# Attention and two mixture layers on one core: the gate tiles are moved by 384 bytes, and TensorE gets filler matmuls in the first stage

## The chip, the cores and the metric

The kernel runs on 1 core of one Trainium2 chip. The metric is the device time of one execution in microseconds (us); the kernel before has a median of 1256.49 us over 3 runs (1256.25 to 1257.84).

## What is computed

The reference is linear attention over 4 batches, 8 heads, 576 positions and 64 channels, then a feed-forward layer on 2304 tokens (512 to 2048 to 512), then four experts (512 to 1024 to 512) whose results are summed with the weights of `domain_probs`. Cut to what matters:

```python
q_s = softmax(q, axis=-1);  k_s = softmax(k, axis=2)
x = q_s @ (k_s.T @ v)                    # per head, heads side by side: 2304 x 512
h = x @ w_in                             # w_in and w_out arrive in float64
g = where(h >= 1, h, where(h <= -1, 0, (h + 1) ** 2 / 4))
x = g @ w_out
for e in range(4):
    out += p[:, e:e+1] * (maximum(x @ w1[e], 0) @ w2[e])
```

## The kernel before, in words

Tokens are cut into five blocks (512, 512, 512, 256, 512). They run in two passes: blocks 1 and 0, then blocks 2, 4 and 3. In each pass the first layer comes first ("a") and the four experts follow ("b"). Each product of two matrices is made of three matmuls of rounded parts, high and low, in `products` (lines 998, 999 and 1000): the low weight part with the high moving part, high with low, high with high. So nearly all of TensorE's time stands under these three lines. Most products of two blocks are made with seven products in place of eight (`strassen`); the first layer of the first pass is made plainly, by `ups` (line 1121 and on).

The hidden values of a step are written as a pair of tiles, high and low, that the program calls gates. `gated` (lines 1322 to 1351) does it for the first layer, `opened` (line 1308 and on) for the experts; then `downs` (line 1353 and on) multiplies them with the second weights. For the first layer a gate is the moving operand and the weight is loaded into the array ("bank<-gate,w" in the trace, moving operand first). For the experts the gate is loaded and the weight moves ("bank<-w,gate").

Three sets of tiles serve as gates. Halves of spare `x` tiles serve at first. Eight tiles named `gate` come when the conversion of the float64 weights is over: `end_conversion` (line 343) closes the pool `convert` and opens the pool `gates` in its place, on the right side of the memory (lines 352 to 354). Ten tiles named `gate_late` come when the attention is over. They lie on the left side.

Where the tiles lie follows from the allocation. Left-side pools are stacked from low addresses up, right-side pools from the top down. In the program before, the tiles `x`, `acc`, `w`, `cv`, `words` and `gate_late` all start 96 bytes past a multiple of 512 in each partition. The right-side pool is 16,384 bytes long and starts at byte 212,960, which is 480 past a multiple of 512. In it lie, first, `words1`, `m1` and `t1` of the conversion, and later the eight `gate` tiles of 2,048 bytes each, so each `gate` tile starts at 480, too.

The first stage holds the attention of batches 0 and 1 (`load_units`, `keys`, `queries`), the conversion of float64 weights on VectorE and ScalarE (`split_double`, lines 675 to 727) and the first steps of the first layer. TensorE's order is not written by hand: every piece of work is a generator that asks for an engine and a cost, for a buffer, or for an event. `Order.run` keeps a clock for each engine in the computed order, and always lets the request go on that can start first; among requests for the same engine that can start within 0.05 of the first, the one with the lowest due number goes. The order found so is the order of the instructions on each engine. `order.now` is the computed time. An estimate of the costs is in the code: a matmul of n columns costs 0.0135 + n / 2400 per pass, and a hop between engines 0.2.

`ups` writes to the banks of `ups_banks`. At first there are two of them (line 359); two more come when batch 1 and when all batches are done. `ups` takes its bank at the start of a step, before its weights and its x are there, and `gated` gives it back after the VectorE instruction of line 1340. A generator that asks for a buffer while one is free gets it at once:

```python
        elif isinstance(want, Bufs) and want.free:
            time, item = want.take()
            self.hold(task, time)
            self.go_on(task, item)
```

In the trace a float32 matmul of the program (as in lines 819, 823, 920 and 921) shows as two records, x2.

Of the kernel before, what the change touches and what calls it, by code (L numbers as in the profile page):

```python
# [8 lines left out]
F32 = mybir.dt.float32  # L9
# [8 lines left out]
P = 128  # L18
EPS = 1e-9

PE, ACT, DVE, POOL, SP = "PE", "ACT", "DVE", "POOL", "SP"
# [155 lines left out]
def act(n, psum=False):  # L177
    return ACT, (0.14 if psum else 0.17) + n * 0.00087


def dve(n):
    return DVE, 0.14 + n * 0.00107
# [15 lines left out]
def attention_moe_kernel(  # L198
# [12 lines left out]
    nc = tc.nc  # L211
# [43 lines left out]
    steps = [(g, j) for g, (bi, ws) in enumerate(groups) for j in range(len(ws))]  # L255
# [18 lines left out]
    QRATIO = 9.0  # L274
    MARGIN = 0.5
    POOLRATIO = 3.0
    CORDER = range(KC)

    def bufs(pool, n, shape, dtype, name):
        return [pool.tile(shape, dtype, name=f"{name}{i}") for i in range(n)]  # L280
# [5 lines left out]
    ident = const.tile([P, P], F32, name="ident")  # L286
# [18 lines left out]
    for i, (_, n) in enumerate(blocks):  # L305
# [12 lines left out]
    at_first = convert.enter_context(tc.tile_pool(name="convert", bufs=1, side="right"))  # L318
# [5 lines left out]
             xtiles.pop()),  # L324
        )
    ])
    xfree = Bufs([])
    first_gates = [(x[:, i * 512:(i + 1) * 512], x) for x in xtiles for i in range(2)]
    gate_home = {id(g): x for g, x in first_gates}
# [4 lines left out]
    def give_gate(g, t):  # L334
        x = gate_home.get(id(g))
        if not switched or x is None:
            gates.put(g, t)
        elif id(x) in halves_in:
            xfree.put(x, max(t, halves_in.pop(id(x))))
        else:  # L340
            halves_in[id(x)] = t

    def end_conversion(t):

        switched.append(True)
        free, gates.free = gates.free, []
        for t0, _, g in free:
            give_gate(g, max(t, t0))
        for t0, _, x in made_of.free:
            xfree.put(x["f"], max(t, t0))  # L350
        convert.close()
        pool = ctx.enter_context(tc.tile_pool(name="gates", bufs=1, side="right"))
        for x in bufs(pool, 8, [P, 512], F32R, "gate"):
            gates.put(x, t)
        for i in range(3):
            raws.put(words[:, i * 512:(i + 1) * 512], t)

    banks = bufs(psum, 8, [P, 512], F32, "bank")
    ups_banks = Bufs(banks[:2])
# [61 lines left out]
    order = Order()  # L421

    def end_attention(t):
        early.close()
        late = ctx.enter_context(tc.tile_pool(name="late", bufs=1))
        for x in bufs(late, 10, [P, 512], F32R, "gate_late"):
            gates.put(x, t)
        ups_banks.put(banks[6], t)
# [14 lines left out]
    def token_rows(t, t0, n):  # L443

        done = 0
        while done < n:
            b, s = divmod(t0 + done, S)
            place, p = (1 + s // P, s % P) if s < (NC - 1) * P else (0, s - (NC - 1) * P)
            m = min(n - done, HP - p % HP)
            rows = t[b * S:(b + 1) * S]  # L450
            if p < HP:
                rows = rows[:HP * NC].rearrange("(p c) d -> c p d", c=NC)[place, p:p + m]
            else:
                p -= HP
                rows = rows[HP * NC:].rearrange("(p c) d -> c p d", c=NC - 1)[place - 1, p:p + m]
            yield done, m, rows
            done += m
# [3 lines left out]
    def norm_probs():  # L461
        start = Event()
        start.set(150.0)
        yield start
        for i in range(NT // P):
            for o, n, rows in token_rows(probs, i * P, P):
                t = yield SP, 0.65
                nc.sync.dma_start(out=pn[o:o + n, i, :], in_=rows)
        late = Event()
        late.set(t + 3)  # L470
        yield late
        t = yield dve(300)
        nc.vector.tensor_reduce(out=psum_p, in_=pn, axis=AX.X, op=ALU.add)
        nc.vector.tensor_scalar(out=psum_p, in0=psum_p, scalar1=EPS, scalar2=None, op0=ALU.add)
        nc.vector.reciprocal(out=psum_p, in_=psum_p)
        nc.vector.tensor_tensor(
            out=pn, in0=pn, in1=psum_p.unsqueeze(2).to_broadcast([P, NT // P, NE]), op=ALU.mult
        )
        probs_in.set(t)
# [21 lines left out]
    def load_weights():  # L501
        for ws in jobs:
            w = ws[0]
            yield step_of[w][0]
            if is_kept(w):
                for h in range(2):
                    for w in ws:
                        raw = yield raws
                        raw_of[w, h] = raw
                        t = yield SP, 0.48  # L510
                        nc.sync.dma_start(
                            out=f32(raw).rearrange("p (z n) -> p z n", z=2), in_=kept[w[:3]][:, :, h]
                        )
                        loaded[w, h].set(order.arrival(t, 4096))
                continue
            kind, e, f = w[:3]
            n = P * len(ws)
            both = (yield wide_raws) if kind == "a" else None
            a, c = (w_in, w_out) if kind == "a" else (w1[e], w2[e])
            fs = slice(f, f + n)  # L520
            for h, src in enumerate((
                a[:, fs].rearrange("(c p) f -> p c f", p=P), c[fs].rearrange("(c p) d -> p c d", p=P)
            )):
                if kind == "a":
                    raw_of[w] = both
                    raw = both[:, h * 512:(h + 1) * 512]
                else:
                    raw_of[w, h] = yield raws
                    raw = f32(raw_of[w, h])
                t = yield SP, 0.48  # L530
                nc.sync.dma_start(
                    out=raw.rearrange("p (c f) -> p c f", c=KC if h == 0 else len(ws)), in_=src
                )
                loaded[w, h].set(order.arrival(t, 4096))
# [140 lines left out]
    def split_double(w, cv):  # L675
# [49 lines left out]
        if not to_convert:  # L725
            end_conversion(at_time)
# [45 lines left out]
    def load_units():  # L772
        for b, hp in todo:
            yield att_due[b, hp] - 0.1
            hs = slice(2 * hp, 2 * hp + 2)
            if (b, hp) == (1, 0):
                yield GATE
            if (b, hp) == (NOW, 0):
                yield calm
            small = yield k_small  # L780
            kt = yield wide
            k_at = Event()
            k_at.set((yield from load(places(kt), k[b, hs])))
            ek = yield wide
            order.add(keys(b, hp, small, kt, ek, k_at), "att", att_due[b, hp])
            small = yield q_small
            qt = yield wide
            q_at = Event()
            q_at.set((yield from load(places(qt), q[b, hs])))
            order.add(queries(b, hp, small, qt, q_at), "att", att_due[b, hp])  # L790

    def keys(b, hp, small, kt_buf, ek_buf, k_at):
# [39 lines left out]
        else:  # L832
            yield pe(P, 2)
            nc.tensor.transpose(bank[:, P:2 * P], mc.to_broadcast([P, P]), ident)
            rows, way = bank[:, P:2 * P], dve(W)
            if order.busier(DVE, POOL, POOLRATIO):
                t, e = yield [act(P, True), dve(P)]
# [56 lines left out]
    def queries(b, hp, small, qt_buf, q_at):  # L894
# [98 lines left out]
        if len(done) == len(todo):  # L993
            end_attention(t)


    def products(ps, ah, al, bh, bl, first, last, **kw):
        nc.tensor.matmul(ps, al, bh, start=first, stop=False, **kw)  # L998
        nc.tensor.matmul(ps, ah, bl, start=False, stop=False, **kw)  # L999
        nc.tensor.matmul(ps, ah, bh, start=False, stop=last, **kw)  # L1000
# [112 lines left out]
    def prepare_all():  # L1113
        for i in range(len(PASSES)):
            if i:
                yield from prepare(i, "a")
            yield from prepare(i, "b")
# [235 lines left out]
    def downs():  # L1353
        s0 = 0
        for g, (bi, ws) in enumerate(groups):
# [4 lines left out]
            if kind == "a" and bi == PASSES[0][0][1] and g == place[-1]:  # L1360

                each = [x for x in each if x[0] < 2] + [(j, c) for c in CORDER for j in range(2, nj)]
            ps, left, begun = {}, [m] * nj, [0] * m
# [68 lines left out]
    with tc.manual_schedule():  # L1432
        make_identity(nc, ident)
        nc.gpsimd.tensor_scalar(
            out=nident, in0=ident, scalar1=-1.0, scalar2=None, op0=ALU.mult
        )
        nc.gpsimd.memset(half, 0.5)
        nc.scalar.activation(out=one, in_=half, func=AF.Exp, scale=0.0)
        nc.gpsimd.memset(rebias, -8.0 * ((1023 - 127) << 20))
        for free in kvbds:  # L1440
            for _, _, t in free.free:
                nc.gpsimd.memset(t, 0.0)
        order.clock[POOL] = 3.0
        order.add(load_units(), "load")
        order.add(load_weights(), "load")
        order.add(convert_weights(), "conv")
        order.add(downs(), "ffn")
        order.add(ups(), "ffn")
        order.add(prepare_all(), "ffn")
        order.add(norm_probs(), "load", len(steps))  # L1450
        order.run()


# [30 lines left out]
```

## Time and profile before

| | us |
|---|---|
| median of 3 runs | 1256.49 |
| the profiled execution, its own time | 1260.49 |
| its span, first to last instruction | 1258.7 |
| TensorE (PE) busy | 1222.2 (97%) |
| VectorE (DVE) busy | 668.7 (53%) |
| GpSimd (POOL) busy | 568.7 (45%) |
| ScalarE (ACT) busy | 510.7 (41%) |

The page of the profile gives these for one execution. TensorE's matmuls are pipelined, so the duration of one record overlaps the next; the distance from one start to the next tells what a matmul costs. The granted clock of TensorE is given as a share of full speed: 1.00 is 2.4 GHz and 0.50 is 1.2 GHz. Before the first change of the clock that the profile recorded (at about 16 us), the clock column shows 1.00 whatever the clock was.

### The profile page before, as it was taken

To read this page: it belongs to the slowest core of one execution; us is meant where nothing else is said; L and a number is where in the kernel's file an instruction comes from. 1 tells how busy PE (TensorE), PEld (TensorE's weight loads), DVE (VectorE), ACT (ScalarE), POOL (GpSimd) and SP (SyncE) were. 2 spreads that over 40 slices of the span, in tenths; PEclk is the share of its full clock that TensorE was granted. 3 is DMA by queue.
4 is the path that set the end of the run, shared out by engine and by line. 5 is a ranking of instruction groups with operands and counts; after the bars stand their busy time and mean duration, and the time that the engine had idled before them with its cause. 6 is when DMAs were issued, how large, how long until landed. Compare 5 with 4: busy or idle time off the path is not lost.

```text
span 1258.7 us, 15378 instructions
## 1 busy us (share of the span) xinstructions
PE 1222.2 (97%) x5716; PEld 1001.8 (80%) x5716; DVE 668.7 (53%) x1030; ACT 510.7 (41%) x918; POOL 568.7 (45%) x559
## 2 busy tenths in 40 slices
PE   6789999989999999999999999999999999999998
PEld 3568888867778878888788888888888888888886
DVE  5878885467564654445553455673334333343333
ACT  3657765343433433323574443533223223232220
POOL 1323233465744645533673745748334253342500
PEclk9999999999999999999999999999999999999999
DMA  7856754114232212111531221202011010111003
GB/s 184 242 159 201 237 199 151 34 38 119 83 86 86 78 55 78 36 66 35 140 127 67 99 74 63 67 1 72 32 65 34 34 51 22 63 34 34 17 1 84
DMA packets 86218, 105.37 MB, mean 84 GB/s; under 512 B 28544, under 2 KB 61312, under 8 KB 86144
## 3 DMA queue, kind: packets, MB, share of 16 engines
q1 hardware_dynamic: 86144, 104.39, 26.8%
q8 instruction: 45, 0.74, 0.2%
q14 instruction: 29, 0.24, 0.1%
HBM read 82.87 MB, written 21.50 MB: 83 GB/s over the span
## 4 chain that ended last, share of the span: by engine, by line
PE 88%; DVE 5%; DMA 3%; issue 1%; POOL 1%; ACT 1%; SPq 1%; DVEq 0%; POOLq 0%; ACTq 0%
PE bank L998 28%; PE bank L999 28%; PE bank L1000 28%; DMA acc<-in_v_dram 1%; PE bank L867 1%; PE bank L962 1%; DVE acc L440 1%; DMA wide<-in_q_dram 1%; POOL w L440 1%; DMA acc<-in_k_dram 1%; DVE x L440 0%; PE bank L952 0%; DMA acc<-in_q_dram 0%; SPq L758 0%; ACT w L435 0%
## 5 line engine op out<-in xcount | busy, mean ns | idle before, releaser
L998 PE MATMUL bank<-x,w 128*128 128x512 f32 (+1 forms) x988 | 372.6, 377 | 8.0 <-DVE w L710 3.6
L999 PE MATMUL bank<-x,w 128*128 128x512 f32 (+1 forms) x988 | 366.4, 371 | 3.2 <-DVE x L440 1.1
L1000 PE MATMUL bank<-x,w 128*128 128x512 f32 (+1 forms) x988 | 366.0, 370 | 0.0
L440 POOL TENSOR_TENSOR w<-words,w 128x512 fp32r<-128x512 f32 (+1 forms) x128 | 159.3, 1248 | 248.3 <-ACT w L435 247.5
L998 PEld LDWEIGHTS bank<-x,w 128*128 128x128 f32 x988 | 187.0, 189 | 45.6 <-DVE w L710 4.3
L999 PEld LDWEIGHTS bank<-x,w 128*128 128x128 f32 x988 | 187.0, 189 | 37.1 <-DVE x L440 2.2
L1000 PEld LDWEIGHTS bank<-x,w 128*128 128x128 f32 x988 | 186.8, 189 | 31.9
L1422 DVE SCALAR_TENSOR_TENSOR acc<-bank,pn,acc 128x512 f32<-128x512 f32 x126 | 88.6, 749 | 133.7 <-PE bank L1000 133.7
L435 ACT CAST w<-words 128x512 fp32r<-128x512 f32 (+2 forms) x160 | 106.8, 681 | 84.3 <-PE bank L1000 67.1
L998 PE MATMUL bank<-w,gate 128*128 128x512 f32 x344 | 138.6, 403 | 0.6 <-DVE gate L1315 0.6
L999 PE MATMUL bank<-w,gate 128*128 128x512 f32 x344 | 135.7, 394 | 0.0
L1000 PE MATMUL bank<-w,gate 128*128 128x512 f32 x344 | 135.7, 394 | 0.0
L440 POOL TENSOR_TENSOR w<-cv,w 128x512 fp32r<-128x512 f32 x80 | 104.6, 1307 | 39.9 <-ACT w L435 36.9
L440 POOL TENSOR_TENSOR x<-cv,x 128x512 fp32r<-128x512 f32 x28 | 45.2, 1617 | 107.4 <-ACT x L435 79.8
L998 PE MATMUL bank<-w,gate_late 128*128 128x512 f32 x232 | 90.7, 391 | 1.1 <-DVE gate_late L1315 1.1
L1000 PE MATMUL bank<-w,gate_late 128*128 128x512 f32 x232 | 90.5, 390 | 0.0
L999 PE MATMUL bank<-w,gate_late 128*128 128x512 f32 x232 | 90.4, 389 | 0.0
L435 ACT CAST w<-cv 128x512 fp32r<-128x512 f32 x80 | 49.6, 619 | 97.6 <-POOL cv L440 97.4
L1313 ACT ACTIVATE gate<-bank 128x512 fp32r<-128x512 f32 (+1 forms) x74 | 41.3, 558 | 104.6 <-PE bank L1000 62.2
L1227 DVE TENSOR_TENSOR cv<-bank,cv 128x512 f32<-128x512 f32 x40 | 27.6, 690 | 101.1 <-PE bank L1000 101.1
L998 PEld LDWEIGHTS bank<-w,gate 128*128 128x128 f32 x344 | 64.8, 189 | 15.8 <-DVE gate L1315 1.2
L1000 PEld LDWEIGHTS bank<-w,gate 128*128 128x128 f32 x344 | 64.8, 188 | 15.2
(173 smaller groups left out, 1890.5 us busy)
## 6 DMA issues: line engine op xcount, KB each, us to landing
words<-in_moe_w_dram SPq DMA_DIRECT2D x64, 512.0 KB, 3.4
kept<-w SPq DMA_DIRECT2D x32, 512.0 KB, 4.2
words<-kept SPq DMA_DIRECT2D x32, 512.0 KB, 4.0
words<-in_moe_w_in_dram SPq DMA_DIRECT2D x16, 512.0 KB, 4.0
words<-in_moe_w_out_dram SPq DMA_DIRECT2D x16, 512.0 KB, 5.4
out_dram<-acc SPq DMA_DIRECT2D x36, 128.0 KB, 2.4
wide<-in_q_dram SPq DMA_DIRECT2D x22, 160.0 KB, 3.2
wide<-in_k_dram SPq DMA_DIRECT2D x20, 160.0 KB, 3.1
```

Source lines behind the costliest of these rows:

```text
L435: nc.scalar.copy(out=dst, in_=src)
L440: (nc.vector if engine == DVE else nc.gpsimd).tensor_tensor(**kw)
L867: nc.tensor.matmul(bank[:, :N], ek[:, c, :], vt_buf[:, c * N:(c + 1) * N], start=(c == 0), stop=(c == NC - 1),)
L962: nc.tensor.matmul(bank[:, :hi - lo], bd, qt_buf[:, lo:hi], start=True, stop=True)
L998: nc.tensor.matmul(ps, al, bh, start=first, stop=False, **kw)
L999: nc.tensor.matmul(ps, ah, bl, start=False, stop=False, **kw)
L1000: nc.tensor.matmul(ps, ah, bh, start=False, stop=last, **kw)
L1227: nc.vector.tensor_tensor(out=tile["s"], in0=bank, in1=tile["s"], op=ALU.add)
L1313: nc.scalar.activation(out=gh, in_=h, func=AF.Relu)
L1422: nc.vector.scalar_tensor_tensor(out=dst, in0=p, scalar=by, in1=dst, op0=ALU.mult, op1=ALU.add)
```

## The change

Two pools on the right side get a further tile of 96 float32 (384 bytes) that nothing uses, and a further generator, `keep_warm`, asks for TensorE at cost 0.25 as long as the computed time is under 60. Its due number is above that of every step. Each time it gets TensorE it issues one matmul of the identity with itself, 128 columns in float32, to a bank of `ups_banks`; nobody reads the result.

```diff
+    WARM = 60.0
...
+
+    at_first.tile([P, 96], F32, name="pad")
     xfree = Bufs([])
...
         for x in bufs(pool, 8, [P, 512], F32R, "gate"):
             gates.put(x, t)
+        pool.tile([P, 96], F32, name="pad_late")
...
+    def keep_warm():
+
+        while order.now < WARM:
+            bank = yield ups_banks
+            t = yield PE, 0.25
+            nc.tensor.matmul(bank[:, :P], ident, ident, start=True, stop=True)
+            ups_banks.put(bank, t)
...
         order.add(norm_probs(), "load", len(steps))
+        order.add(keep_warm(), "warm", 10 * len(steps))
         order.run()
```

## Rows read from the trace of the kernel before

**Rows 1.** The page: TensorE's busy tenths and granted clock, 40 slices of 31.5 us.

```profile
PE   6789999989999999999999999999999999999998
...
PEclk9999999999999999999999999999999999999999
```

**Rows 2.** Busy time by stretch: us, PE, PEld, DVE, ACT, POOL busy (x), clock, DMA share, GB/s.

```profile
0.00:70.00 70.00, 51.10 (x203) 32.75 (x203) 48.85 (x107) 36.39 (x95) 20.77 (x42) 0.93 0.74 196
70.00:100.00 30.00, 25.99 (x114) 20.18 (x115) 21.61 (x31) 16.96 (x32) 5.20 (x8) 0.94 0.49 160
100.00:1258.00 1158.00, 1145.12 (x5401) 948.92 (x5400) 598.28 (x894) 457.31 (x792) 542.77 (x510) 1.00 0.24 75
```

**Rows 3.** TensorE's groups by line and shape, line 999: busy us, mean ns | idle before.

```profile
L999 PE MATMUL bank<-w,gate 128*128 128x512 f32 x344 | 135.7, 394 | 0.0
...
L999 PE MATMUL bank<-w,gate_late 128*128 128x512 f32 x232 | 90.4, 389 | 0.0
...
L999 PE MATMUL bank<-gate,w 128*128 128x512 f32 x76 | 29.9, 394 | 0.0
...
L999 PE MATMUL bank<-gate_late,w 128*128 128x512 f32 x72 | 28.2, 392 | 0.0
```

**Rows 4.** TensorE's timeline, first and last of three unbroken runs: 59, 24 and 36 matmuls.

```profile
388.74 0.39 PE L999 MATMUL bank<-w,gate 128*128 128x512 f32 x1
...
402.22 0.39 PE L1000 MATMUL bank<-w,gate 128*128 128x512 f32 x1
...
231.50 0.40 PE L998 MATMUL bank<-gate,w 128*128 128x512 f32 x1
...
236.87 0.39 PE L1000 MATMUL bank<-gate,w 128*128 128x512 f32 x1
...
971.87 0.40 PE L998 MATMUL bank<-w,gate_late 128*128 128x512 f32 x1
...
979.83 0.40 PE L1000 MATMUL bank<-w,gate_late 128*128 128x512 f32 x1
```

**Rows 5.** The chain that ended last, pieces up to 83 us: start us, us, what.

```profile
15.62 6.80 DMA acc<-in_v_dram
...
22.98 2.32 PE bank L867 x10
25.30 0.43 PE bank L819 x2
...
26.16 1.17 PE bank L819 x2
27.33 0.86 PE bank L823 x2
...
28.62 0.22 PE bank L920 x2
...
81.90 1.12 PE bank L867 x10
```

**Rows 6.** Busy time by stretch (columns as in rows 2), two stretches at the low clock.

```profile
23.30:26.60 3.30, 3.30 (x15) 2.99 (x14) 3.20 (x6) 0.37 (x2) 2.37 (x2) 0.50 0.00 0
...
60.80:64.20 3.40, 3.40 (x9) 2.65 (x8) 2.23 (x7) 1.48 (x4) 0.00 (x0) 0.50 0.65 202
```

**Rows 7.** TensorE's timeline around the second step of ups, 60 to 66 us.

```profile
60.49 0.56 PE L998 MATMUL bank<-x,w 128*128 128x512 f32 x1 [2.00 <-DVE w L710]
60.85 0.63 PE L999 MATMUL bank<-x,w 128*128 128x512 f32 x1
...
62.99 1.05 PE L962 MATMUL bank<-wide,kvbd 128*128 128x256 f32 x2
...
65.41 0.28 PE L809 MATMUL bank<-ident,mk 128*128 128x128 f32 x1
```

**Rows 8.** VectorE's timeline: the instruction that gives the first step's bank back.

```profile
67.73 0.68 DVE L1340 TENSOR_TENSOR cv<-bank,cv 128x512 f32<-128x512 f32 x1
```

## The prediction

> **What bounds the kernel now.** I read the page first. TensorE is busy 9 tenths or more in nearly every slice, and the slices below that stand almost all in the first stage [rows 1]. The busy time by stretch says the same in three numbers [rows 2]: TensorE is busy 51.1 of the first 70 us, 26.0 of the next 30, and 1145.1 of the 1158 us behind them. So from 100 us on TensorE sets the end. There every nanosecond that a matmul loses or gains is seen at the end, but for at most 1158 - 1145.1 = 12.9 us of idle time (in which the few missing records are counted, too). In the first 70 us TensorE waits for 18.9 us. What happens there counts only as far as it moves the moment at which TensorE's work becomes unbroken.
>
> Then I read the matmuls themselves, by shape [rows 3] and by the distance of their starts [rows 4]. Of 128x512 matmuls with a `gate` tile there are 344 on each of the three lines with the gate loaded, and 76 on each with the gate moving. The reader is to see a difference that durations hint at (394 ns against 389) and that starts show well: 58 steps from 388.74 to 402.22 us are 232.4 ns each with `gate`; 35 steps from 971.87 to 979.83 us are 227.4 ns each with `gate_late`. Shape, lines and moving operand are the same. With the gate as the moving operand, 23 steps from 231.50 to 236.87 us are 233.5 ns each.
>
> Last I read the chain that ended last in the first stage [rows 5]. Up to 22.4 us it hangs on the transfers of k and v, then it runs over TensorE from 22.98 us.
>
> **Part one, the 384 bytes.** The two new tiles make both right-side pools 384 bytes longer, so their start goes from byte 212,960 to 212,576. That is 96 past a multiple of 512, where `x`, `w` and `gate_late` are. In the trace of before the one thing in which `gate` differs from `gate_late` is its place, so I take it that a `gate` matmul will cost what a `gate_late` matmul costs. Gate loaded: 3 x 344 = 1032 matmuls by 232.4 - 227.4 = 5.0 ns give 5.2 us. Gate moving: 3 x 76 = 228 by 233.5 - 227.4 = 6.1 ns give 1.4 us. Together **6.6 us**, all of it behind 100 us, on the engine that sets the end. The bounds: zero, if the place is not the cause; 1260 x 6.1 ns = 7.7 us, if the larger step is true of all. The number of `gate` tiles against `gate_late` ones may change with the order, by a few tens of matmuls, which is some tenths of a us. The conversion's `words1`, `m1` and `t1` move by the same 384 bytes; the tiles of the other set lie at 96 already and serve the same instructions, so I cost that at nothing. If it costs something, it lies on VectorE in the first stage.
>
> **Part two, the fillers.** The nearest row to a filler is line 920 with 128 columns: 0.22 us at the full clock; line 819 at half clock took 0.43 [rows 5]. The computed order charges 0.25. The number is not shown by a trace; TensorE's idle time before 70 us gives an estimate: 18.9 / 0.25 = 76 fillers, 16.7 us at full clock. They replace idle time where the computed gap is a real one. Where TensorE is late against the computed order, they delay what is behind them, by 0.22 each.
>
> What can be won: the stretches at the low clock [rows 6] that lie on the chain. From 22.98 us ten matmuls of line 867 took 2.32 us, where at full clock they took 1.12: 1.2. Two pairs of 0.43 would take 0.22: 0.4. The 1.17 of line 819 against the 0.86 of line 823 beside it: 0.3. Sum 1.9 us. From 60.85 us five matmuls of 128x512 took 2.14 us [rows 7]; at 227 ns each they take 1.13: 1.0; the 1.2 us of low clock behind them give back at most half: 0.6. Sum 1.6 us. So at most 3.5 us, if all of it reaches the end. I doubt that. Ahead of 22.98 us TensorE stands idle for v [rows 5], and line 867 is queued there behind nothing that the order sees as free; fillers stand only where the computed order has a gap. And VectorE and the transfers, which hold the chain between 30 and 60 us, do not get faster.
>
> What can be lost: the fillers take one of the two banks. The generator puts its bank back and takes it again at once, so the second step of `ups` can't have it while fillers run. That step began at 60.49 us, and waited for a weight until then [rows 7]. Now it must wait until the first step's bank is given back, at 67.73 + 0.68 = 68.41 us [rows 8], unless the fillers end before. This is a wait that the change adds: 7.9 us at most. Behind the waiting matmul TensorE's queue holds the attention of batch 1 (lines 962, 809), but the computed order knows of the wait and puts those first. That helps: line 809 at 65.41 us stood behind the step's twelve matmuls, and line 1340 is in the queue of VectorE behind work that waits for line 809. So the bank may come back earlier than 68.41, and the step's work falls into idle time that TensorE had there.
>
> I set part two at **0**, between -3.5 and +5. What stays of either sign at 70 us meets 4 us of idle time between 70 and 100 us [rows 2], which takes up a part of a loss and cuts a gain short.
>
> **The sum.** The profiled execution took 1260.5 us, 1.8 over its span, and 4.0 over the median. Less 6.6 it is 1253.9. Against the median of 1256.5: 1256.5 - 6.6 + 0 = **1249.9 us**. What is late next is again TensorE, at 227 ns a matmul.
>
> **Rivals.** One: the place doesn't matter, and the `gate` tiles are slow for another reason, such as being the highest in memory, which they stay. For it: matmuls with `gate` are the only ones that read there. Against it: nothing in the trace gives height a price either. Then the time is 1256.5 with part two at nothing. Chance 0.12. The Trainium skill's page "SBUF — State Buffer" (section "Who interferes with whom") speaks for this rival: by it TensorE's moving operand and its weights come through two independent read ports, and TensorE never waits on anyone; by that rule alone the first term would be zero and the sum 1256.5. The rows disagree with a rule by which all places cost the same: 232.4 against 227.4 ns [rows 4].
>
> Two, the other side: the bank. If the order doesn't get the attention out of the way, the second step of `ups` goes from 60.49 to 68.41 us and everything behind it with it: 7.9 us. Eleven fillers in the slot of 2.7 us that its twelve matmuls leave empty (12 x 227 ns, at 0.25 each) add 11 x 0.22 = 2.4. Price 10.3, less 6.6: 1260.2 us. It ends above the time of before by more than 0.2% if the unbroken work starts over 6.6 + 2.5 = 9.1 us later. Against it: 4 us of idle time stand between 70 and 100 us [rows 2], and TensorE waits for VectorE's weights there, not for this step alone. Chance 0.07.
>
> Three: the clock stays up, and all of it reaches the end, with the dip of the clock between 90 and 100 us (0.94 between 70 and 100 us in [rows 2], 30 x 0.06 / 0.5 = 3.6 us at half clock, 1.8 lost) gone as well: 1256.5 - 6.6 - 3.5 - 1.8 = 1244.6. Chance 0.08: fillers end at 60 of computed time, so this dip is not theirs to fill.
>
> **How the numbers follow.** The forecast, gates faster and the first stage within some us of before, has 0.73. Its own range is 1246.4 (part two -3.5) to 1254.9 (+5). The range for 8 in 10 reaches a little to both sides, 1245 to 1255.5; it leaves out rival two, most of rival one and a part of rival three. A measurement of this kernel can tell about 0.2%, 2.5 us, from no change. Faster by more than that (under 1254.0): nearly all of the forecast, rival three and a little of one: 0.82. Within: most of rival one, a little of the forecast and of two: 0.12. Slower: the rest, 0.06.
>
> **What would show it.** Right: matmuls with `gate` start every 227 ns, loaded and moving, and their count is near 1260. TensorE's work is unbroken from about 90 us. Some 70 to 100 fillers stand before 70 us, of 0.22 us, most of them ahead of a wait. The second step of `ups` starts behind line 1340 of the first step. Wrong: `gate` stays at 232 ns; or the unbroken work begins at 95 us or later, or at 86 or earlier; or a new wait of more than 3 us appears behind 100 us because the order has changed.

## The result: 10.2 us less, of which the place of the gate tiles gives two thirds

The changed kernel takes 1246.2 us (median of 4 runs, 1244.31 to 1247.28), the kernel before in the same comparison 1256.37 (4 runs, 1256.09 to 1257.84). The ratio is 0.9915, with a 95% interval of 0.9898 to 0.9932. That is 10.2 us less; the forecast was 6.6 us less, and its range held the time, 1.2 us above its lower end. Of the executions told below one is far off and left out of its ratio: with the fillers alone, 1524.84 us at a mean granted clock of 0.752.

The page of the changed kernel, TensorE's busy tenths and its granted clock (against [rows 1]):

```profile
PE   8989999999999999999999999999999999999998
...
PEclk9999999999999999999999999999999999999999
```

Busy time by stretch of the changed kernel (columns as in [rows 2]), and below it the fillers alone in the first stretch (PE and PEld):

```profile
0.00:70.00 70.00, 63.62 (x375) 50.29 (x375) 51.16 (x112) 37.26 (x98) 21.12 (x43) 1.00 0.71 199
70.00:100.00 30.00, 26.21 (x123) 20.69 (x122) 26.61 (x34) 22.24 (x39) 4.88 (x7) 1.00 0.67 225
100.00:1243.00 1143.00, 1130.77 (x5373) 942.90 (x5371) 585.66 (x885) 449.57 (x784) 537.86 (x510) 1.00 0.24 74
...
0.00:70.00 70.00, 21.88 (x150) 20.45 (x150) 1.00 0.71 199
```

The fillers are 150 records, which is 75 matmuls of the program. The clock of the first two stretches went from 0.93 and 0.94 to 1.00. Behind 100 us idle time is 12.2 us as against 12.9.

TensorE's timeline of the changed kernel, first and last of the runs that answer to the first two of [rows 4] (59 and 24 matmuls):

```profile
379.93 0.39 PE L1011 MATMUL bank<-w,gate 128*128 128x512 f32 x1
...
393.10 0.39 PE L1012 MATMUL bank<-w,gate 128*128 128x512 f32 x1
...
224.75 0.39 PE L1010 MATMUL bank<-gate,w 128*128 128x512 f32 x1
...
229.97 0.39 PE L1012 MATMUL bank<-gate,w 128*128 128x512 f32 x1
```

The steps are 13.17 / 58 = 227.1 ns and 5.22 / 23 = 227.0 ns; before they were 232.4 and 233.5. All other matmuls of that shape still take 227 ns. The matmuls of 128x256 with a moving `gate` did not pay before, and gain nothing: they start every 119 ns before and every 120 now (means of 79 steps each).

To part the two effects I use one instruction that stands in all these kernels behind the first stage and ahead of most `gate` matmuls: the matmul of the first layer's end that waits 0.65 us for VectorE's `x`. Its row in the trace of before, and in that of the changed kernel:

```profile
259.38 0.50 PE L999 MATMUL bank<-x,w 128*128 128x512 f32 x1 [0.65 <-DVE x L440]
```

```profile
252.24 0.50 PE L1011 MATMUL bank<-x,w 128*128 128x512 f32 x1 [0.66 <-DVE x L444]
```

Ahead of it the changed kernel is 7.1 us faster in these two executions; behind it the span has 1258.7 - 259.4 = 999.3 us before, and 1243.8 - 252.2 = 991.6 us now, 7.7 less. The sum, 14.9 us, is more than the medians' 10.2, chiefly because the profiled execution of before was a long one (1260.49 us against a median of 1256.49).

TensorE's timeline of the changed kernel at the start and around the second step of `ups`:

```profile
1.36 6.09 PE L1005 MATMUL bank<-ident 128*128 128x128 f32 x38 [1.36 <-POOL ident masks.py:199]
7.29 0.27 PE L813 MATMUL bank<-ident,mk 128*128 128x128 f32 x1
7.39 1.06 PE L1005 MATMUL bank<-ident 128*128 128x128 f32 x8
8.29 1.02 PE L823 MATMUL bank<-acc,ident 128*128 128x512 f32 x2
...
22.83 1.39 PE L871 MATMUL bank<-acc 128*128 128x130 f32 x10 [1.90 <-POOL acc L865]
...
57.87 2.05 PE L1005 MATMUL bank<-ident 128*128 128x128 f32 x16
59.68 0.48 PE L1010 MATMUL bank<-x,w 128*128 128x512 f32 x1
```

the first row of the old line 819 in the trace of before:

```profile
7.28 2.08 PE L819 MATMUL bank<-acc,ident 128*128 128x512 f32 x2 [0.92 <-DVE mc L811]
```

and, in the changed kernel again, VectorE's instruction that gives back the first step's bank (against [rows 8]):

```profile
55.69 0.67 DVE L1352 TENSOR_TENSOR cv<-bank,cv 128x512 f32<-128x512 f32 x1
```

The first 38 records are 6.09 us of matmuls at the start, where TensorE had nothing to do. Line 823 of 512 columns, the old line 819, takes 1.02 us for its two records there at 8.29 us; before, the first two took 2.08 us. But the matmuls that wait for v (line 871, the old 867) start at 22.83 us, against 22.98 before: all that was gained ahead of them is 0.15 us. They themselves take 1.39 us in place of 2.32. The first step's bank comes back at 56.36 us, 12 us earlier than before, and the second step of `ups` starts at 59.68, behind it.

### The profile page after: what moved, and what is told of

Its sections match the earlier page's. It is cut to its first block, busy times and chain, and to the rows that moved or that the text cites. A ratio compares the mean times of both kernels' runs of the same rounds, so it can differ in the third digit from the quotient of the medians.

```text
span 1243.8 us, 15689 instructions
## 1 busy us (share of the span) xinstructions
PE 1220.6 (98%) x5866; PEld 1013.9 (82%) x5866; DVE 663.4 (53%) x1030; ACT 509.1 (41%) x918; POOL 563.9 (45%) x559
## 4 chain that ended last, share of the span: by engine, by line
PE 89%; DVE 4%; DMA 2%; POOL 2%; issue 1%; ACT 1%; SPq 1%; POOLq 0%; DVEq 0%; ACTq 0%
PE bank L1010 28%; PE bank L1011 28%; PE bank L1012 28%; PE bank L871 1%; PE bank L966 1%; DMA acc<-in_k_dram 1%; POOL cv L444 1%; POOL w L444 1%; DMA acc<-in_v_dram 1%; PE bank L956 1%; DVE acc L444 1%; POOL x L444 0%; PE bank L1005 0%; DMA words<-kept 0%; DVE x L444 0%
## 5 line engine op out<-in xcount | busy, mean ns | idle before, releaser
L1010 PE MATMUL bank<-w,gate 128*128 128x512 f32 x344 | 137.1, 399 | 0.0
L1012 PE MATMUL bank<-w,gate 128*128 128x512 f32 x344 | 134.1, 390 | 0.0
L1011 PE MATMUL bank<-w,gate 128*128 128x512 f32 x344 | 134.1, 390 | 0.0
L444 POOL TENSOR_TENSOR x<-cv,x 128x512 fp32r<-128x512 f32 x28 | 40.7, 1456 | 104.4 <-ACT x L439 88.6
```

The source lines that it names most:

```text
L444: (nc.vector if engine == DVE else nc.gpsimd).tensor_tensor(**kw)
```

## The experiments

All times below are medians; the kernel before was run along in each comparison. Where a table needs it, "mark" is the start of the instruction with the wait of 0.65 us told above, and "behind" is the span less the mark.

**The pads alone**

```diff
-        order.add(keep_warm(), "warm", 10 * len(steps))
```

> The two 384-byte tiles alone, no fillers; the order is that of before. Theory (the place of the gate tiles costs 5 to 6 ns in each of 1260 matmuls): gate matmuls start every 227 ns, the clock falls to half in the first 100 us as before, and the time is 1256.4 - 8 = 1248.4 us (8.0 is what the changed kernel gained on the one before behind 225 us). Rival (the fillers carry the gain, by their order or by the clock): 1256 us, within 2 us of before.

Measured: 1250.44 us, ratio 0.9943 (0.9927 to 0.9960), 7.4 us less. The order of all engines is that of before. Its mark:

```profile
255.91 0.50 PE L1011 MATMUL bank<-x,w 128*128 128x512 f32 x1 [0.65 <-DVE x L444]
```

Behind it are 1248.8 - 255.9 = 992.9 us, 6.4 less than the 999.3 of before. The steps of `gate` matmuls are 227 ns. So the place alone gives 6 to 7 us, and it gives them where the matmuls with `gate` stand. The mark is 3.5 us earlier, too, in the same order; only 60 of the 1260 matmuls stand ahead of it, some 0.3 us, and the clock of the two executions differs there (0.95 and 0.95 with the pads, 0.93 and 0.94 before).

**The fillers alone**

```diff
-    at_first.tile([P, 96], F32, name="pad")
...
-        pool.tile([P, 96], F32, name="pad_late")
```

> The fillers alone, the gate tiles at the old place. Theory: gate matmuls start every 232 ns, and the first stage gives what the two medians leave, 10.2 - 8.0 = 2.2 us: 1254.2 us. Rival (the first stage is worth the 6.8 us by which the changed kernel was ahead at 225 us in the two profiled executions): 1249.6 us.

Measured: 1253.11 us, ratio 0.9961 (0.9949 to 0.9973), 4.9 us less by the ratio: between the two expectations. TensorE's timeline of this run, the run of 59 matmuls with `gate` again, and the mark:

```profile
381.29 0.39 PE L1009 MATMUL bank<-w,gate 128*128 128x512 f32 x1
...
394.76 0.39 PE L1010 MATMUL bank<-w,gate 128*128 128x512 f32 x1
```

```profile
254.08 0.50 PE L1009 MATMUL bank<-x,w 128*128 128x512 f32 x1 [0.66 <-DVE x L442]
```

13.47 / 58 = 232.2 ns: without the pads the matmuls stay slow. The mark is 5.3 us earlier than before, and behind it there are still 997.2 us. So each part does its own: the pads behind the mark, the fillers ahead of it.

**The new order without the fillers**

```diff
             t = yield PE, 0.25
-            nc.tensor.matmul(bank[:, :P], ident, ident, start=True, stop=True)
```

> As the changed kernel, but the fillers only take their time in the computed order and are not issued: the order of all other instructions is that of the changed kernel, TensorE's clock is left alone. If the clock is what the fillers bring: the clock falls to half in the first 100 us again, and the time is that of the pads alone, 1248.4 us. Rival, the new order (the second step of ups behind the attention) brings it: 1246.2 us as the changed kernel, or less, since 16 us of filler matmuls are gone.

Measured: 1249.11 us, ratio 0.9927 (0.9902 to 0.9953). The six runs go from 1243.0 to 1252.6, a wider range than that of any of the runs above. Busy time by stretch in the profiled one (1251.15 us):

```profile
0.00:70.00 70.00, 51.28 (x215) 32.98 (x216) 49.92 (x109) 35.33 (x95) 21.61 (x42) 0.93 0.69 195
70.00:100.00 30.00, 25.49 (x110) 20.10 (x109) 23.58 (x34) 19.01 (x34) 3.97 (x7) 0.89 0.63 197
```

The clock falls as before (0.93 and 0.89), and the mark is at 257.3 us, 5.1 later than in the changed kernel. One of the six runs had a mean clock of 0.999 over its whole span, and that one took 1243.0 us, less than any run of the changed kernel. The other five had 0.990 to 0.993: three of them took 1251.2 to 1252.6 us, but two, both at 0.992, took 1246.2 and 1247.1, as the changed kernel does. The interval does not tell this kernel from the pads alone nor from the changed kernel. So the mean clock over a span does not say what its falls cost, and with one of the six runs traced it is not shown what set the two groups apart.

**All tiles at 480**

```diff
+    const.tile([P, 96], F32, name="shift")
     ident = const.tile([P, P], F32, name="ident")
```

(in the kernel before; nothing else of the change)

> The kernel before with 384 further bytes at the start of the left side: x, w, cv, acc and gate_late now lie 480 past a multiple of 512, where the gate tiles lie, too; no fillers. Theory (what costs is that the two operands lie at different places): gate matmuls 227 ns as all others, 1248.4 us as with the pads. Rival (480 is slow by itself, as it is 32 bytes ahead of a multiple): all matmuls of 128x512 at 232 ns or more, about 4000 x 5 ns = 20 us more, 1276 us. Rival (the gates are slow because they lie highest in memory): gate matmuls stay at 232 ns, 1256 us.

Measured: 1250.18 us, ratio 0.9941 (0.9922 to 0.9961). The run of 59 matmuls again:

```profile
382.19 0.40 PE L1000 MATMUL bank<-w,gate 128*128 128x512 f32 x1
...
395.34 0.39 PE L1001 MATMUL bank<-w,gate 128*128 128x512 f32 x1
```

13.15 / 58 = 226.7 ns. The gate tiles lie at the same addresses as before, highest in memory and 480 past a multiple of 512. What moved is everything else. So neither the height nor the 480 is what costs: it is that TensorE's loaded and moving operands lie at different places. Both rivals fall, and with them rival one of the prediction.

**Eight places, first try**

```diff
-        for x in bufs(pool, 8, [P, 512], F32R, "gate"):
-            gates.put(x, t)
-        pool.tile([P, 96], F32, name="pad_late")
+        for letter, after in zip("abcdefgh", (8, 8, 16, 32, 32, 8, 24, 96)):
+            gates.put(pool.tile([P, 512], F32R, name=f"gate_{letter}"), t)
+            pool.tile([P, after], F32, name=f"pad_{letter}")
```

> As the changed kernel, but the eight gate tiles have names of their own (gate_a to gate_h) and start 96, 128, 160, 224, 352, 480, 0 and 96 past a multiple of 512; gate_a and gate_h differ by half a period of 1024. If the period is 512 bytes: matmuls with gate_a and gate_h start every 227 ns, those with the six others more slowly, up to 233. If it is 256: gate_e (352) is as fast. If it is 1024: gate_a (96 past a multiple of 1024, where all other tiles are at 608) is slow and gate_h is fast. With six of eight tiles off the place, the time is some 5 us over the changed kernel's.

Measured: 1249.36 us in one run, and no clear answer by tile. The 98 steps from one matmul that loads gate_a, at the common place, to the next that does are 232.3 ns on average. The program always uses the tiles in pairs (a with b, c with d, and so on), a matmul with the one stands beside a matmul with the other, and here the two of a pair lay at different places. The tile's own place did not protect gate_a. By pairs the steps of the loaded gate are 232.4, 232.3, 231.3 and 231.9 ns: all four are slow.

The trace of before points the same way. In 20 places a matmul that loads `gate_late`, with both operands at the common place, is followed by one that loads `gate`; these steps are 232.4 ns on average, and 226.6 with the pads. So more counts than the two operands of one matmul: what the next matmul loads counts, too. Which of the reads meet each other is not shown. The next experiment puts both tiles of a pair at one place.

**Four places, by pairs**

```diff
-        for x in bufs(pool, 8, [P, 512], F32R, "gate"):
-            gates.put(x, t)
-        pool.tile([P, 96], F32, name="pad_late")
+        for letter, after in zip("abcdefgh", (0, 32, 0, 32, 0, 72, 0, 88)):
+            gates.put(pool.tile([P, 512], F32R, name=f"gate_{letter}"), t)
+            if after:
+                pool.tile([P, after], F32, name=f"pad_{letter}")
```

> As the changed kernel, but the gate tiles lie in four pairs (a pair is what one step uses): gate_a and gate_b 96 past a multiple of 512, gate_c and gate_d 224, gate_e and gate_f 352, gate_g and gate_h 128. Theory (a matmul is slower where the two operands lie at different places within 512 bytes): 227 ns a step with the first pair, 231 to 235 with the three others. If the period were 256, the third pair would be at 227 as well; if it were 128, the second and the third.

Measured: 1253.37 us in one run, with the clock at 0.98 and 0.94 in the two first stretches. TensorE's timeline, first and last of a run of 12 matmuls with each pair, in the order a and b (96), c and d (224), e and f (352), g and h (128):

```profile
287.84 0.39 PE L1011 MATMUL bank<-w,gate_b 128*128 128x512 f32 x1
...
290.34 0.39 PE L1013 MATMUL bank<-w,gate_a 128*128 128x512 f32 x1
...
423.14 0.40 PE L1011 MATMUL bank<-w,gate_d 128*128 128x512 f32 x1
...
425.70 0.40 PE L1013 MATMUL bank<-w,gate_c 128*128 128x512 f32 x1
...
340.53 0.39 PE L1011 MATMUL bank<-w,gate_f 128*128 128x512 f32 x1
...
343.03 0.39 PE L1013 MATMUL bank<-w,gate_e 128*128 128x512 f32 x1
...
337.74 0.39 PE L1011 MATMUL bank<-w,gate_h 128*128 128x512 f32 x1
...
340.30 0.40 PE L1013 MATMUL bank<-w,gate_g 128*128 128x512 f32 x1
```

By 11 steps each: 227, 233, 227 and 233 ns. Over all such runs of the gate as the loaded operand (18, 18, 13 and 15 of them) the means are 227.7, 232.9, 227.2 and 232.9 ns. The pair at 352, which is 96 + 256, is as fast as the pair at 96. So the place counts within 256 bytes, not 512: the theory is right in kind, and its period was wrong.

**A filler that holds no bank**

```diff
-            bank = yield ups_banks
             t = yield PE, 0.25
-            nc.tensor.matmul(bank[:, :P], ident, ident, start=True, stop=True)
-            ups_banks.put(bank, t)
+            free = [x for x in ups_banks.free if x[0] <= t - 0.25]
+            if free:
+                e = min(free, key=lambda x: x[:2])
+                nc.tensor.matmul(e[2][:, :P], ident, ident, start=True, stop=True)
+                ups_banks.free.remove(e)
+                ups_banks.put(e[2], t)
```

> As the changed kernel, but a filler holds no bank while it waits for TensorE: it takes one only if one lies free at that moment, and otherwise is not issued. The second step of ups can take its bank early, as before. If the wait for the bank cost something in the changed kernel: faster than its 1246.2 us, by up to 3 us. If the fillers bring the clock and the wait costs nothing: no fillers while both banks are taken (some 46 to 58 of computed time), the clock falls there again, and the time is 1247 to 1250 us.

Measured: 1246.91 us (1243.63 to 1247.71), ratio 0.9912 (0.9895 to 0.9928): as the changed kernel, with 134 records of fillers in place of 150. In the profiled run the clock was 0.98 and 0.94 in the two first stretches, lower than the changed kernel's, so two effects may cancel in it. What can be said is that the wait for the bank neither costs nor brings anything that can be told by the time.

**Fillers for longer, and for less long**

```diff
-    WARM = 60.0
+    WARM = 100.0
```

> WARM = 100 instead of 60. If what is left of low clock in the changed kernel (0.996 to 1.0 of the span in its four runs, up to 10 us at half clock in the worst) lies behind 60 of computed time: the clock stays at 0.999 or above in all runs, and the time is 1244.5 us with less spread. Rival, the fillers are in the way of work that has become ready (TensorE is nearly full there), and the bank is missed longer: 1247 us or more.

> WARM = 20: only the fillers ahead of the first matmul and in the gaps behind it, about 54 of the 150 records. If the clock in the very first stretch is what counts: 1246 us as the changed kernel. If it is the later falls (between 45 and 75 us): the clock falls there as with the pads alone, and the time is near theirs, 1249 to 1250.5 us.

(the second with `WARM = 20.0`)

Measured: 1254.48 us, ratio 0.9971 (0.9959 to 0.9982), for 100, and 1253.69, ratio 0.9975 (0.9961 to 0.9988), for 20. Both are far worse than the changed kernel, and worse than the pads alone: for 100 as its rival had it, for 20 outside both of its expectations. Their marks are at 258.5 and 261.8 us, 6.3 and 9.6 later than the changed kernel's, and behind those stand 990.4 and 990.3 us, as little as in any kernel with pads. So the time is lost ahead of the mark. With 100 the clock isn't why: it stood at 1.00 in both of the first stretches. But TensorE had no idle time left between 70 and 100 us, and 72 records of fillers took 8.84 us there, in which no other matmul ran:

```profile
70.00:100.00 30.00, 30.00 (x180) 26.30 (x179) 25.68 (x35) 21.30 (x36) 4.68 (x6) 1.00 0.66 225
```

With 20 the clock was 0.98 and 0.89 in the two stretches, no better than with the pads alone. Then there are new waits between 100 us and the mark, 2.5 us with 100 and 5.6 with 20. These rows the changed kernel does not have, first with 100, then with 20 (us in total, times, longest):

```profile
PE bank L1010 <- ACT gate L439: 1.6, 1, 1.6
...
PE bank L1011 <- POOL gate L444: 0.9, 1, 0.9
```

```profile
PE bank L1010 <- ACT x L439: 3.0, 2, 2.8
...
PE bank L1010 <- DVE cv L1352: 1.7, 1, 1.7
...
PE bank L1010 <- DVE w L714: 0.9, 1, 0.9
```

A filler that takes time in the computed order moves the work behind it, and the order from there on is another one. In the changed kernel that went well; these two show that it need not, and the one with 100 that fillers cost time where TensorE has work.

**Fillers in the order of before**

```diff
+            if HELD[e][0] == PE:
+                self.fill(self.clock[PE], start)
...
+    def fill(a, b):
+        lent = [x for f in (ups_banks, att_banks[-1]) for x in f.free if x[0] <= a]
+        if a < WARM and lent:
+            bank = min(lent, key=lambda x: x[:2])[2]
+            for _ in range(int((b - a) / 0.25)):
+                nc.tensor.matmul(bank[:, :P], ident, ident, start=True, stop=True)
...
-        order.add(keep_warm(), "warm", 10 * len(steps))
+        order.fill = fill
```

> The pads, the order of the kernel before on all engines, and 52 fillers put into TensorE's gaps of the computed order up to 60, into banks that lie free there; the fillers cost nothing in the computed order. If the clock is what the fillers bring: low clock in the first 100 us goes down from about 20 us to 15 or less, and the time is 1247 us against 1250.4 with the pads alone. If the new order is needed: 1250 us.

> As the run before with fillers up to 100 of computed time (60 of them); the order stays that of the kernel before. In the run with WARM = 100 a new order cost waits behind 100 us; here there can be none. Expected: the same or up to 2 us less than with fillers up to 60, 1245 to 1247 us. Rival: fillers ahead of work that is ready cost as much as the clock gives, 1248 us or more.

(the second with `WARM = 100.0`)

Measured: 1249.0 us, ratio 0.9936 (0.9917 to 0.9954), and 1247.87 us, ratio 0.9925 (0.9907 to 0.9943). Each lies between what its two readings expected. Busy time by stretch of the first of them:

```profile
0.00:70.00 70.00, 58.38 (x314) 43.94 (x315) 51.52 (x111) 37.69 (x97) 22.71 (x44) 0.99 0.74 199
70.00:100.00 30.00, 27.52 (x127) 22.17 (x126) 21.70 (x31) 19.96 (x35) 4.38 (x5) 0.96 0.61 192
```

With the order of before and the clock at 0.99 and 0.96, the mark is at 254.6 us, 1.3 earlier than with the pads alone (whose clock is 0.95 and 0.95). With fillers to 100 it is at 254.3. By the medians the gain over the pads is 1.4 and 2.6 us, which the intervals don't settle. The changed kernel's mark, 252.2 us, was not reached.

**The changed kernel with 8 fillers more**

```diff
+        if WARM <= a < 100.0 and lent:
```

(the generator of the change up to 60, and `fill` as above between 60 and 100)

> The changed kernel with 8 further fillers, put into TensorE's gaps of the computed order between 60 and 100 into a bank that lies free, at no cost in the computed order, so that the order stays that of the changed kernel. If the rest of the low clock lies there and can be reached: 1245 us, and 0.998 or more in all runs. If not (8 fillers of 0.22 us are too few for the gaps that stand there): 1246.2 us as the changed kernel, with falls of the clock between 69 and 85 us in some runs.

Measured: 1245.78 us (1243.97 to 1247.61), ratio 0.9910 (0.9893 to 0.9928). That cannot be told from the changed kernel. No version here is surely better than it.

The marks side by side, each from one profiled execution:

| kernel | clock 0 to 70 | clock 70 to 100 | mark, us | behind, us |
|---|---|---|---|---|
| before | 0.93 | 0.94 | 259.4 | 999.3 |
| pads alone | 0.95 | 0.95 | 255.9 | 992.9 |
| all at 480 | 0.97 | 0.96 | 255.1 | 991.1 |
| pads, fillers to 60, order of before | 0.99 | 0.96 | 254.6 | 990.5 |
| pads, new order, no fillers | 0.93 | 0.89 | 257.3 | 992.1 |
| fillers alone | 0.98 | 1.00 | 254.1 | 997.2 |
| changed kernel | 1.00 | 1.00 | 252.2 | 991.6 |
| changed kernel, fillers hold no bank | 0.98 | 0.94 | 254.4 | 991.5 |
| changed kernel, 8 fillers more | 1.00 | 0.94 | 254.1 | 990.4 |
| pads, fillers to 100, order of before | 0.98 | 1.00 | 254.3 | 990.9 |
| changed kernel, fillers to 100 | 1.00 | 1.00 | 258.5 | 990.4 |
| changed kernel, fillers to 20 | 0.98 | 0.89 | 261.8 | 990.3 |

The column behind the mark has two values: 997 to 999 where the gate tiles lie elsewhere than the other tiles, 990 to 993 where they lie at the same place. The mark follows the clock, by and large, but for the last two rows, whose other losses were told above (the clock column does not show how long the low clock of the very start lasted).

## Why the prediction was right, and where its sum was off

**The place of the gate tiles: right.** 6.6 us were forecast, from the step of `gate_late`. The pads alone gave 7.4 us by the medians, and 6.4 us behind the mark, in the same order. The step of 227 ns came out to the nanosecond for both roles of the gate. The count of matmuls did not change. The argument, that place was the one thing in which the two sets of tiles differ, held; the run with all tiles at 480 shows that it is the difference of places that costs. The Trainium skill's page "SBUF — State Buffer" (section "Who interferes with whom") says that TensorE's two read ports are independent and that it waits on no one. The trace does not agree for TensorE's own loaded and moving operands: 232.4 ns against 226.7 ns at the same gate addresses.

**The fillers: the sign was open, and the size was off.** "I set part two at 0, between -3.5 and +5" is the term that was mis-sized. By the gains part two is 10.2 - 7.4 = 2.8 us (4.2 by the medians of the two kernels themselves), and the fillers alone gave 4.9 (3.4 to 6.4), by the middle of the interval more than the 3.5 that I had as the most. Two steps failed in it. I let the falls of the clock at 23 and at 91 us stay, since no filler stands there; in the profiled run of the changed kernel the clock did not fall once (the means of its other three runs are 0.996 to 0.999). And I took the gain as cut short by idle time between 70 and 100 us. It was not: TensorE's last wait before its work becomes unbroken ends 6.2 us earlier. Here it is before, and in the changed kernel:

```profile
90.37 0.50 PE L999 MATMUL bank<-x,w 128*128 128x512 f32 x1 [0.91 <-ACT w L435]
```

```profile
84.13 0.70 PE L966 MATMUL bank<-acc,kvbd 128*128 128x256 f32 x2 [1.50 <-ACT kvbd L888]
```

That is one of the prediction's own signs of being wrong ("at 86 or earlier"), and it came up. What happened in the first stage is near rival three, in which the clock stays up and all of it reaches the end: it gave 1244.6 us and had a chance of 0.08. The median is 1.6 us above it and 3.7 below the forecast. That the early low clock, ahead of the transfers of v, was counted as nothing did no harm: its end brought the matmuls behind v forward by 0.15 us only.

**The number of fillers: right.** The estimate of 76 met 75, and the cost of 0.22 us each is what the records show (0.11 us for each of the two).

**The bank (rival two): did not happen.** The step of `ups` waits for the bank as said, but the computed order puts the attention first, as the prediction held against the rival. Line 1340 (now 1352) runs at 55.69 us in place of 67.73, and the step starts at 59.68, 0.8 us earlier than before. The run in which a filler holds no bank takes the same time.

**What of the cause stays open.** Whether the new order has a worth of its own. The order alone gave a ratio of 0.9927, with the clock falling in the profiled run, the order of before with fillers gave 0.9936 and 0.9925; the intervals overlap. In two pairs of rows of the table with about the same loss of clock the new order has the earlier mark (8 fillers more against the fillers to 60 in the order of before, 254.1 to 254.6; no bank held against all at 480, 254.4 to 255.1), but these are single executions. That the fillers' part comes through the clock rests on three things: the fillers without the pads move the mark by 5.3 us and what stands behind it by 2.1; over the kernels of the table the mark follows the clock, by and large; and with the new order the one run with the clock at 0.999 was the fastest of six by 3.2 us. Against it stand the two runs at 0.992 that took no longer than the changed kernel. So it is argued with support, and not shown; how the gain is shared between clock and order is not measured.

## What to carry to other kernels

When matmuls of one shape take two different times, compare the addresses of their operands: the remedy here was 384 unused bytes. Fill an idle TensorE in a lead-in to keep its clock up, but look at what else the filler moves: in a kernel whose order is computed, a filler that takes time there draws a new order, and one that stands where TensorE has work holds it up; the same idea with other limits (20 or 100 in place of 60) lost 7 us by the ratios. Part two effects with a mark in the trace that both kernels share, before you add up medians.

## What the runs showed of the hardware that was not expected

A matmul of 128x512 in this kernel takes 227 ns from start to start if the loaded and the moving operands start at the same place within 256 bytes, and 232 to 233 ns if they differ by 32, 128 or 384 bytes; a difference of 256 costs nothing. It is the same whichever of the two is the gate. Where the two tiles of a pair lie at different places, the one at the common place is slow, too (232 ns in the first try). Matmuls of 128x256 with the gate moving show no such cost (119 ns before, 120 with the pads).

The mean granted clock differs from run to run of one kernel: over the 16 runs of the kernel before that stood beside the pads, it was 0.992 to 0.996 over the span. The three at 0.992 took 1259.3 to 1259.5 us, the one at 0.996 took 1254.0. All 16 lie between 1254.0 and 1260.5 us. The mean does not fix the time, though: of the 11 runs of the same kernel that stood beside the four places, one at 0.997 took 1259.5 us.
